# Three attention steps of TensorE issued as one task from the seventh chunk on, and fewer filler matmuls

## The chip, the core and the metric

The kernel runs on one core of a Trainium2 chip. The metric is device microseconds of one execution. The kernel before takes 482.16 us, the median of 3 runs (481.86 to 482.75). Everything is in one program on the core's engines: TensorE (PE, with its weight loads shown apart as PEld), VectorE (DVE), ScalarE (ACT), GpSimd (POOL), and the DMA queue that SyncE (SP) issues to.

## What is computed

Three layers, on 4 batches of 768 tokens with 384 channels (8 heads of 48). Cut to what matters:

```python
# 1. linear attention with decay, per batch and head
for t in range(768):
    cur = einsum('d,e->de', u * k[t], v[t])
    y[t] = r[t] @ (state + cur)
    state = w[:, None] * state + einsum('d,e->de', k[t], v[t])
# 2. gated MLP with a product over tokens
h = gelu(x @ w_in);  u, v = halves of h (512 each)
v_n = (v - mean) / sqrt(var + 1e-6) * g_ln
x = x + (u * (w_sg @ v_n + b_sg)) @ w_out
# 3. gated convolution
gate = sigmoid(causal conv of x, 5 taps per channel)
out = (gate * (x @ w_val)) @ w_out2
```

## The kernel before

The attention runs in 24 chunks of 128 tokens (chunk i is chunk i % 6 of batch i // 6). For each chunk TensorE does these steps, with the names that the rows use:

- T (`att_T`, L536): eight transposes, r and k of the chunk, each into its own PSUM bank; DVE and ACT scale and copy them out as `rT` and `kT`.
- S (`att_S`, L557): the scores, 8 products `kT` by `rT` with 48 rows contracted, into two PSUM banks. DVE masks them into two tiles `sc` (L565).
- KV (`att_KV`, L579): the chunk's state product, 8 products of k and v, 48 x 48 each. DVE adds the old state (L588), ACT decays it (L594).
- Y (`att_Y`), three parts into one bank: four transposes of the diagonal term `dv` (L612), the old state times `rT` (L619), and scores times v (L624), 8 products with 48 output rows. ACT copies the bank out (L637), and a DMA writes and re-reads it in the layout of the next layer.

L557 uses 48 rows of the array (its operands are 48 partitions high), L624 and L579 fill 48 of its columns; every other matmul of the kernel uses 112 or 128 rows and columns. A float32 matmul appears in the trace as two records, so that the 8 products of L624 are "x16" there.

The two other layers are matmuls in three passes (`three`, L778 to L780), since each float32 operand is split into a high and a low part: V and U (x by w_in, tile names `win`), SG (the product over tokens, `wsg` and `vh`, in f16), O1 (`wout`), VAL (`w_val`) and O2 (`w_out`). They are called the MLP below.

All instructions of a program are laid down in advance by a planner (`go`, L146), which keeps a clock of its own with an assumed duration for every step. There are two streams of PE tasks, attention and MLP, each a list of generators; a `yield` says how long the next piece of a task is taken to last, which results it waits for, and which PSUM banks or buffers it takes. Up to WA = 3 attention tasks and WM = 4 MLP tasks are open at once, the first ready one of each stream is a candidate, and `choose` takes the attention's as long as its share of PE time is under a goal. When neither is ready, the planner moves its clock on, and before FILL_END it lays filler matmuls into the hole (L167 to L170: `onesb` by `onesb` into columns of the bank `pw`, whose other columns hold scratch of the weight conversion, L338 to L341). The work of the other engines is kept as chains of steps, and planned with the same clock. On the chip every engine then executes its own list in order, and waits by semaphore for what it needs.

The attention's tasks stand in the list in the order S(i), KV(i), T(i+1), Y(i) (`attention`, L735; ORDER = "SKTY"). Four PSUM banks `pa` serve the attention, three banks `pm` the MLP.

Of the kernel before, what the change touches and what calls it, by code (L numbers as in the profile page):

```python
# [17 lines left out]
B, H, S, D = 4, 8, 768, 48  # L18
DM = H * D
FF = 512  # L20
NCH = S // P
# [9 lines left out]
class Kern:  # L31
# [114 lines left out]
    def go(self, streams, choose):  # L146

        live = [[] for _ in streams]
        self.done = [0.0] * len(streams)
        while True:  # L150
            for n, (gens, window) in enumerate(streams):
                while len(live[n]) < window and gens:
                    g = gens.pop(0)
                    live[n].append([g, next(g)])
            if not any(live):
                return
            times = [[self.when(t[1][2], t[1][1], self.now) for t in ts] for ts in live]
            ready = [next((i for i, t in enumerate(ts) if t is not None and t <= self.now), None) for ts in times]
            n = choose(ready)
            if n is None:  # L160
                best = self.next_step()
                soon = [t for ts in times for t in ts if t is not None]
                if best is not None:
                    soon.append(max(best[0][0], self.now))
                assert soon, ("stuck", [t[1] for ts in live for t in ts], [(c[3], c[5], c[4][0][3:]) for c in self.chains])
                t = min(soon)
                for _ in range(int((t - self.now) * (FILL0 if self.now < 14000 else FILL) / (112 if self.now < 4000 else 56)) if self.now < FILL_END and min(self.tok["pw"], default=t) <= self.now else 0):  # L167

                    nc = self.nc
                    nc.tensor.matmul(self.pw[:, TH:], self.onesb, self.onesb, start=True, stop=True)  # L170
                self.now = self.pe_end = t
                self.advance(self.now)
                continue
            i = ready[n]
            g, (ns, after, taken) = live[n][i]
            self.take(taken)
            self.pe_end = self.now + ns
            req = next(g, None)
            if req is None:
                live[n].pop(i)  # L180
            else:
                live[n][i][1] = req
            self.done[n] += ns
            self.now = self.pe_end
            self.advance(self.now)
# [338 lines left out]
    def att_T(self, i):  # L524

        nc = self.nc
        res = self.kr[i] = [None, None]
        for n, (src, tab, tag) in enumerate(((self.rp, self.tabR, "rT"), (self.ks, self.tabK, "kT"))):
            old = [("S", i - 1)] if i and n else [("Y", i - 2)] if i > 1 else []

            done = n and i
            yield 430, [("ld", i) if not n else ("kS", i) if i else "k0"] + ([("dT", i - 2)] if i > 1 else []), ["pa"]
            pt = self.ps_a()
            sv = (src[(i + (not i)) % 2] if n else src[i % NL]).rearrange("t h d -> t (h d)")
            for p in range(NP):
                nc.tensor.transpose(pt[:HR, p * P:(p + 1) * P], sv[:, p * P:p * P + HR], self.ident)  # L536
            pv = pt[:HR, :].rearrange("d (p t) -> d p t", t=P)

            def evac(e, pv=pv, tab=tab, tag=tag, n=n, done=done):
                dst = self.wp.tile([HR, NP, P], F32, tag=tag, name=self.nm(tag), bufs=1 if n else 2)  # L540
                if done:
                    e.copy(dst, pv)
                else:
                    e.tensor_mul(dst, pv, tab)  # L544
                res[n] = dst

            self.chain((tag, i), ("A", 620.0, evac, [], ["pa"]) if done else ("V", 660.0, evac, [], ["pa"]), after=old + [("tabR", "tabK")[n]], prio=pr(i))
        self.mark(("T", i))

    def att_S(self, i):  # L550
        nc = self.nc
        yield 1100, [("rT", i), ("kT", i)], ["pa", "pa"]
        rT, kT = self.kr[i]
        pA, pB = self.ps_a(), self.ps_a()
        for p in range(NP):
            for ps, r0 in ((pA, 0), (pB, 64)):
                nc.tensor.matmul(ps[:, p * P:(p + 1) * P], kT[r0:r0 + D, p, :], rT[r0:r0 + D, p, :], start=True, stop=True)  # L557
        self.mark(("S", i))
        mb = self.mask.unsqueeze(1).to_broadcast([P, NP, P])
        parts = self.scores[i] = []  # L560
        for n, ps in enumerate((pA, pB)):

            def masked(e, ps=ps):
                t = self.wp.tile([P, NP, P], F32, tag="sc", name=self.nm("sc"), bufs=2)
                e.tensor_mul(t, ps.rearrange("s (p t) -> s p t", t=P), mb)  # L565
                parts.append(t)

            self.chain(("sc", i, n), ("V", 602.0, masked, ["sc"], ["pa"]), after=[("Y", i - 1)] if i else [], prio=pr(i))

    def att_KV(self, i):  # L570

        nc = self.nc
        c = i % NCH
        yield 520, [("kS", i), ("lv", i)], ["pa"]
        kS, vt = self.kS.get(i), self.vt[i]
        pk = self.ps_a()
        for p in range(NP):
# [26 lines left out]
    def att_Y(self, i):  # L604

        nc = self.nc
        b, c = divmod(i, NCH)
        yield 430, [("D", i)], ["pa"]
        py = self.ps_a()
        dv = self.dvp[i % 2].rearrange("t h d -> t (h d)")  # L610
        for p in range(NP):
# [2 lines left out]
        rT = self.kr[i][0]  # L614
        if c:
            yield 880, [("kv", i - 1)], []
            T = self.T[i % 2]
            for p in range(NP):
                nc.tensor.matmul(py[:HR, p * P:(p + 1) * P], T[:, p, :], rT[:, p, :], start=False, stop=False)  # L619
        yield 1000, [("sc", i, 0), ("sc", i, 1)], []  # L620
        sc = self.scores.pop(i)
        for p in range(NP):
            for j, r0 in ((0, 0), (1, 64)):
# [2 lines left out]
        self.mark(("Y", i))  # L626
        self.give("sc", 2)
        self.x_rows(b, c, py[:HR], self.xd[i])

    def x_rows(self, b, c, py, scr):  # L630

# [103 lines left out]
    def attention(self):  # L735

        out = [self.att_T(0)]
        n = B * NCH
        for i in range(n):
            step = {  # L740
                "S": [self.att_S(i)] + ([] if i else [self.tables_state()]),
                "K": [self.att_KV(i)] if i % NCH != NCH - 1 else [],
                "T": [self.att_T(i + 1)] if i + 1 < n else [],
                "Y": [self.att_Y(i)],
            }
            for k in ORDER:
                out += step[k]
        return out + [self.count()]
# [385 lines left out]
def pr(i):  # L1134

    return 0 if i < NCH else PR_A
# [1 line left out]

PR_A, PR_V, PR_V0, PR_U, PR_SG, PR_REST = 1, 0.05, -1, 0.2, 0.8, 2
PR_PS = 1  # L1140
ORDER = "SKTY"
AFTER_SG, AFTER_SM, AFTER_CW = 6, 6, 9
WA, WM = 3, 4
NW = 3
# [9 lines left out]
HOLD_G, HOLD_S, TURN = 200.0, 0.0, 1280.0  # L1154
HOLD = {"gelu": HOLD_G, "sigmoid": HOLD_S}
FILL, FILL0 = 0.4, 0.8
FILL_END = 130000.0
TAIL = [(1, 0, 0), (1, 0, 1), (1, 0, 2), (0, 1, 0), (0, 1, 1), (0, 1, 2), (2, 0, 0), (2, 0, 1), (1, 1, 0), (1, 1, 1), (1, 1, 2), (2, 0, 2), (2, 1, 0), (2, 1, 1), (2, 1, 2)]
W_LEAST, W_MOST = 0.75, 1.0
N_OK = HR * NP  # L1160
# [42 lines left out]
```

## Time and profile before

| | |
|---|---|
| median of 3 runs | 482.16 us |
| the profiled execution | 481.0 us, of it 479.3 us span |
| PE busy | 453.2 us (95%) |
| DVE busy | 344.0 us (72%) |
| ACT, POOL busy | 208.1 us (43%), 175.1 us (37%) |
| chain that ended last | PE 77%, DVE 11%, issue 2%, ACT 2%, POOL 2% |

All parts that follow speak of the profiled execution, whose span is the time between its first and its last instruction. Matmuls are pipelined: a row's duration reaches beyond the start of the next row, so what a matmul costs on PE is the distance from its start to the next start. A row of the timeline merges instructions of one kind that follow each other; its count is at the end. Behind some rows stands the idle time before it and which instruction ended that idle time, inferred from semaphores.

### The profile page before, as it was taken

How to read it: one execution, taken by the hardware profiler on the slowest of the kernel's cores; microseconds unless marked ns; L12 is line 12 of the kernel's file. 1: busy time of each engine (PE TensorE's matmuls, PEld its weight loads, DVE VectorE, ACT ScalarE, POOL GpSimd, SP SyncE). 2: the span in 40 equal slices, each digit the busy share in tenths (PEclk: the TensorE clock that was granted, in tenths of full speed). 3: DMA queues.
4: the chain of work that ended last, by engine and by line, in shares of the span. 5: the costliest groups of instructions: out<-in, count | busy, mean ns of one | idle time of the engine just before them, and what ended most of it. 6: DMA issues, size and time to landing. Idle time of an engine off the chain costs nothing.

```text
span 479.3 us, 8929 instructions
## 1 busy us (share of the span) xinstructions
PE 453.2 (95%) x3423; PEld 380.2 (79%) x3423; DVE 344.0 (72%) x693; ACT 208.1 (43%) x446; POOL 175.1 (37%) x212
## 2 busy tenths in 40 slices
PE   6874989899999999999999999999999989999996
PEld 5763877868777988877887898887777978868796
DVE  5697789898998794536787585577368682658982
ACT  3437658643443475443351554453022354413142
POOL 5755466543465234353343353452023013200000
PEclk9799899999999999999999999999999999999999
DMA  7999775886343323313133433011001201000002
GB/s 148 226 207 314 214 163 110 148 173 199 83 83 74 109 48 93 76 36 83 34 63 80 106 86 112 21 31 34 2 1 41 92 0 51 0 2 0 1 35 72
DMA packets 116274, 41.37 MB, mean 86 GB/s; under 512 B 89345, under 2 KB 114049, under 8 KB 116225
## 3 DMA queue, kind: packets, MB, share of 16 engines
q1 hardware_dynamic: 116224, 40.73, 35.4%
q8 instruction: 29, 0.48, 0.4%
q14 instruction: 21, 0.16, 0.1%
HBM read 28.92 MB, written 9.44 MB: 80 GB/s over the span
## 4 chain that ended last, share of the span: by engine, by line
PE 77%; DVE 11%; issue 2%; ACT 2%; POOL 2%; DVEq 0%; ACTq 0%; POOLq 0%
PE pm L778 22%; PE pm L780 20%; PE pm L779 20%; PE pa L624 4%; PE pa L557 3%; PE pa L536 3%; PE pa L619 3%; PE pa L612 2%; DVE R L679 1%; PE pa L579 1%; DVE sc L565 1%; DVE S L341 1%; DVE bst L817 1%; DVE S L339 1%; DVE S L340 1%
## 5 line engine op out<-in xcount | busy, mean ns | idle before, releaser
L778 PE MATMUL pm<-wsg,vh 128*128 128x384 f16 x192 | 62.9, 328 | 0.0
L780 PE MATMUL pm<-wsg,vh 128*128 128x384 f16 x192 | 62.6, 326 | 0.0
L779 PE MATMUL pm<-wsg,vh 128*128 128x384 f16 x192 | 62.6, 326 | 0.0
L899 DVE SCALAR_TENSOR_TENSOR warm<-xf,cw,warm 128x384 f32<-128x384 f32 x72 | 44.5, 618 | 9.6 <-ACT warm L897 8.4
L565 DVE TENSOR_TENSOR sc<-pa,mask 128x512 f32<-128x512 f32 x48 | 31.5, 683 | 14.8 <-PE pa L557 13.2
L865 DVE SCALAR_TENSOR_TENSOR S<-pm,gs,b_bc 128x384 f32<-128x384 f32 x32 | 19.7, 615 | 28.1 <-PE pm L780 28.0
L520 POOL TENSOR_TENSOR dv<-v,dd 128x384 f32<-128x384 f32 x24 | 20.9, 872 | 49.6 <-DVE dd L513 47.2
L496 POOL TENSOR_TENSOR ks<-kp,tabS 128x384 f32<-128x384 f32 x24 | 25.5, 1064 | 27.6 <-PE pa L579 21.5
L778 PE MATMUL pm<-R,win 128*128 128x384 f32 x96 | 35.2, 366 | 0.0
L778 PE MATMUL pm<-R,wout 128*128 128x384 f32 x96 | 34.2, 356 | 0.0
L835 ACT ACTIVATE S<-pm 128x384 f32<-128x384 f32 x32 | 15.6, 488 | 39.7 <-PE pm L780 39.6
L843 POOL TENSOR_TENSOR R<-xf,R 128x384 fp32r<-128x384 f32 x11 | 11.1, 1010 | 59.2 <-ACT R L1131 37.7
L594 ACT ACTIVATE T<-T,W 112x112 f32<-112x112 f32 x80 | 26.6, 380 | 13.6 <-DVE T L588 13.5
L515 POOL TENSOR_TENSOR dv<-rp,kp 128x384 f32<-128x384 f32 x24 | 25.9, 1078 | 17.9 <-PE pa L612 15.9
L779 PE MATMUL pm<-R,wout 128*128 128x384 f32 x96 | 32.4, 337 | 0.0
L780 PE MATMUL pm<-R,win 128*128 128x384 f32 x96 | 32.4, 337 | 0.0
L779 PE MATMUL pm<-R,win 128*128 128x384 f32 x96 | 32.3, 336 | 0.0
L780 PE MATMUL pm<-R,wout 128*128 128x384 f32 x96 | 32.3, 336 | 0.0
L557 PE MATMUL pa<-rT,kT 48*128 48x128 f32 x384 | 28.8, 291 | 3.6 <-DVE kT L544 2.1
L557 PEld LDWEIGHTS pa<-rT,kT 48*128 48x128 f32 x384 | 24.1, 193 | 9.7 <-issue 4.0
L817 DVE BATCH_NORM_STATS2 bst<-A 128x6 f32<-128x512 f32 x24 | 16.6, 690 | 19.8 <-ACT A L816 19.7
L778 PE MATMUL pm<-win,R 128*128 128x512 f32 x72 | 30.0, 417 | 0.1
(170 smaller groups left out, 1225.4 us busy)
## 6 DMA issues: line engine op xcount, KB each, us to landing
rp<-in_r_dram SPq DMA_DIRECT2D x24, 192.0 KB, 3.5
kp<-in_k_dram SPq DMA_DIRECT2D x24, 192.0 KB, 3.8
v<-in_v_dram SPq DMA_DIRECT2D x24, 192.0 KB, 2.7
xd<-yT SPq DMA_DIRECT2D x48, 96.0 KB, 2.4
xf<-xd SPq DMA_DIRECT2D x24, 192.0 KB, 2.7
out_dram<-S SPq DMA_DIRECT2D x24, 192.0 KB, 2.0
Rst<-in_moe_w_in_dram SPq DMA_DIRECT2D x8, 384.0 KB, 6.0
Rst<-in_moe_w_out_dram SPq DMA_DIRECT2D x7, 384.0 KB, 5.3
```

The lines of the kernel that those rows point to most:

```text
L496: e.tensor_mul(t[:, :, 0:D], kp, self.tabS)
L515: self.chain(("dv", i), ("P", 956.0, lambda e: e.tensor_mul(dv, rp, kp)), after=[("ld", i)] + ([("dT", i - 2)] if i > 1 else []), prio=pr(i))
L520: ("P", 788.0, lambda e: e.tensor_mul(dv, self.vt[i], x["dd"].unsqueeze(2).to_broadcast([P, H, D]))),
L557: nc.tensor.matmul(ps[:, p * P:(p + 1) * P], kT[r0:r0 + D, p, :], rT[r0:r0 + D, p, :], start=True, stop=True)
L565: e.tensor_mul(t, ps.rearrange("s (p t) -> s p t", t=P), mb)
L594: return lambda e: e.activation(tnew[:, p, :], tnew[:, p, :], AF.Copy, scale=self.W[:, p:p + 1])
L778: nc.tensor.matmul(ps, lh, rh, start=m == 0, stop=False)
L779: nc.tensor.matmul(ps, lh, rl, start=False, stop=False)
L780: nc.tensor.matmul(ps, ll, rh, start=False, stop=m == total - 1)
L817: ("V", 602.0, lambda e: e.bn_stats(st, ge)),
L865: ("V", 529.0, lambda e: e.scalar_tensor_tensor(t, pg[:, :TH], self.gs[:, d:d + 1], self.b_bc[:, ts], ALU.mult, ALU.add), [], ["pm"]),
L899: eng.scalar_tensor_tensor(t, row[:, j:j + TH], self.cw[:, e, j:j + 1], t, ALU.mult, ALU.add)
```

## The change

From chunk JOIN = 6 on, Y(i)'s last part (scores times v), KV(i) and S(i+1) are one piece of one task: it waits for everything that the three need, and issues the 8 + 8 + 8 products without anything between. `att_S` is a task of its own up to chunk 6, and `att_KV` up to chunk 5. The last chunk of a batch has no KV, and the last chunk of all has no S behind it. For later chunks T(i) waits for Y(i-2) where it waited for the transposes of `dv` of chunk i-2, and the transposes of `dv` of chunk i wait for Y(i-1). Fillers are laid only while the planner's clock is under 9 us (it was 130 us), and no longer ask whether `pw` is free.

```diff
--- before.py
+++ after.py
@@ -164,7 +164,7 @@
                     soon.append(max(best[0][0], self.now))
                 assert soon, ("stuck", [t[1] for ts in live for t in ts], [(c[3], c[5], c[4][0][3:]) for c in self.chains])
                 t = min(soon)
-                for _ in range(int((t - self.now) * (FILL0 if self.now < 14000 else FILL) / (112 if self.now < 4000 else 56)) if self.now < FILL_END and min(self.tok["pw"], default=t) <= self.now else 0):
+                for _ in range(int((t - self.now) * (FILL0 if self.now < 14000 else FILL) / (112 if self.now < 4000 else 56)) if self.now < FILL_END else 0):
 
                     nc = self.nc
                     nc.tensor.matmul(self.pw[:, TH:], self.onesb, self.onesb, start=True, stop=True)
@@ -529,7 +529,7 @@
             old = [("S", i - 1)] if i and n else [("Y", i - 2)] if i > 1 else []
 
             done = n and i
-            yield 430, [("ld", i) if not n else ("kS", i) if i else "k0"] + ([("dT", i - 2)] if i > 1 else []), ["pa"]
+            yield 430, [("ld", i) if not n else ("kS", i) if i else "k0"] + ([("Y" if i > JOIN + 1 else "dT", i - 2)] if i > 1 else []), ["pa"]
             pt = self.ps_a()
             sv = (src[(i + (not i)) % 2] if n else src[i % NL]).rearrange("t h d -> t (h d)")
             for p in range(NP):
@@ -548,8 +548,11 @@
         self.mark(("T", i))
 
     def att_S(self, i):
-        nc = self.nc
         yield 1100, [("rT", i), ("kT", i)], ["pa", "pa"]
+        self.S_products(i)
+
+    def S_products(self, i):
+        nc = self.nc
         rT, kT = self.kr[i]
         pA, pB = self.ps_a(), self.ps_a()
         for p in range(NP):
@@ -568,10 +571,13 @@
             self.chain(("sc", i, n), ("V", 602.0, masked, ["sc"], ["pa"]), after=[("Y", i - 1)] if i else [], prio=pr(i))
 
     def att_KV(self, i):
+        yield 520, [("kS", i), ("lv", i)], ["pa"]
+        self.KV_products(i)
+
+    def KV_products(self, i):
 
         nc = self.nc
         c = i % NCH
-        yield 520, [("kS", i), ("lv", i)], ["pa"]
         kS, vt = self.kS.get(i), self.vt[i]
         pk = self.ps_a()
         for p in range(NP):
@@ -605,7 +611,7 @@
 
         nc = self.nc
         b, c = divmod(i, NCH)
-        yield 430, [("D", i)], ["pa"]
+        yield 430, [("D", i)] + ([("Y", i - 1)] if i > JOIN else []), ["pa"]
         py = self.ps_a()
         dv = self.dvp[i % 2].rearrange("t h d -> t (h d)")
         for p in range(NP):
@@ -617,7 +623,14 @@
             T = self.T[i % 2]
             for p in range(NP):
                 nc.tensor.matmul(py[:HR, p * P:(p + 1) * P], T[:, p, :], rT[:, p, :], start=False, stop=False)
-        yield 1000, [("sc", i, 0), ("sc", i, 1)], []
+
+        kv = i >= JOIN and c != NCH - 1
+        s = i >= JOIN and i + 1 < B * NCH
+        yield (
+            1000 + 390 * kv + 980 * s,
+            [("sc", i, 0), ("sc", i, 1)] + ([("kS", i), ("lv", i)] if kv else []) + ([("rT", i + 1), ("kT", i + 1)] if s else []),
+            ["pa"] * (kv + 2 * s),
+        )
         sc = self.scores.pop(i)
         for p in range(NP):
             for j, r0 in ((0, 0), (1, 64)):
@@ -626,6 +639,10 @@
         self.mark(("Y", i))
         self.give("sc", 2)
         self.x_rows(b, c, py[:HR], self.xd[i])
+        if kv:
+            self.KV_products(i)
+        if s:
+            self.S_products(i + 1)
 
     def x_rows(self, b, c, py, scr):
 
@@ -738,8 +755,8 @@
         n = B * NCH
         for i in range(n):
             step = {
-                "S": [self.att_S(i)] + ([] if i else [self.tables_state()]),
-                "K": [self.att_KV(i)] if i % NCH != NCH - 1 else [],
+                "S": ([self.att_S(i)] if i <= JOIN else []) + ([] if i else [self.tables_state()]),
+                "K": [self.att_KV(i)] if i < JOIN and i % NCH != NCH - 1 else [],
                 "T": [self.att_T(i + 1)] if i + 1 < n else [],
                 "Y": [self.att_Y(i)],
             }
@@ -1138,7 +1155,7 @@
 
 PR_A, PR_V, PR_V0, PR_U, PR_SG, PR_REST = 1, 0.05, -1, 0.2, 0.8, 2
 PR_PS = 1
-ORDER = "SKTY"
+ORDER, JOIN = "SKTY", 6
 AFTER_SG, AFTER_SM, AFTER_CW = 6, 6, 9
 WA, WM = 3, 4
 NW = 3
@@ -1154,7 +1171,7 @@
 HOLD_G, HOLD_S, TURN = 200.0, 0.0, 1280.0
 HOLD = {"gelu": HOLD_G, "sigmoid": HOLD_S}
 FILL, FILL0 = 0.4, 0.8
-FILL_END = 130000.0
+FILL_END = 9000.0
 TAIL = [(1, 0, 0), (1, 0, 1), (1, 0, 2), (0, 1, 0), (0, 1, 1), (0, 1, 2), (2, 0, 0), (2, 0, 1), (1, 1, 0), (1, 1, 1), (1, 1, 2), (2, 0, 2), (2, 1, 0), (2, 1, 1), (2, 1, 2)]
 W_LEAST, W_MOST = 0.75, 1.0
 N_OK = HR * NP
```

Two places in PE's list and one in DVE's show what this moves. First PE in the middle of the program, about chunk 15 (in the trace of before at 213 to 221 us). Of before, `sc`/`v` is Y (L624), `rT`/`kT` is S (L557), `v`/`ks` is KV (L579); the left-out rows are their other products and MLP matmuls:

```order
L780 MATMUL pm_2671<-wsg_182,vh_2186 128x384
L624 MATMUL pa_2659<-sc_2574,v_2309 48x128
...
L778 MATMUL pm_2671<-wsg_182,vh_2185 128x384
...
L557 MATMUL pa_2732<-rT_2631,kT_2651 128x128
...
L778 MATMUL pm_2726<-wsg_182,vh_2185 128x384
...
L579 MATMUL pa_2770<-v_2530,ks_124 48x48 x8
L778 MATMUL pm_2783<-R_2191,win_96 128x384
```

The same place in the changed kernel, whose lines have other numbers (L637 is Y, L585 KV, L560 S, L795 to L797 the MLP):

```order
L797 MATMUL pm_2764<-wsg_182,vh_2183 128x384
L637 MATMUL pa_2755<-sc_2659,v_2479 48x128
...
L585 MATMUL pa_2800<-v_2479,ks_124 48x48 x8
L560 MATMUL pa_2809<-rT_2760,kT_2746 128x128
...
L795 MATMUL pm_2823<-R_2189,win_96 128x384
```

Where Y, S and KV stood between MLP matmuls one by one, they now follow each other. The second place is PE's list at the first chunk, with the fillers (`onesb`), of before:

```order
L579 MATMUL pa_315<-v_143,ks_123 48x48 x8
L612 MATMUL pa_327<-ident,dv_131 112x128 x4
L170 LDWEIGHTS onesb
L170 MATMUL warm<-onesb 128x128
L536 MATMUL pa_337<-ident,rp_118 112x128 x4
...
L624 MATMUL pa_327<-sc_334,v_143 48x128
L170 LDWEIGHTS onesb
...
L536 MATMUL pa_373<-ident,ks_124 112x128 x4
```

and of the changed kernel:

```order
L585 MATMUL pa_315<-v_143,ks_123 48x48 x8
L618 MATMUL pa_327<-ident,dv_131 112x128 x4
L536 MATMUL pa_336<-ident,rp_118 112x128 x4
L637 MATMUL pa_327<-sc_324,v_143 48x128
...
L536 MATMUL pa_365<-ident,ks_124 112x128 x4
```

All eight fillers of this place are gone. Three more go later (two ahead of chunk 3's `dv`, one in the T of chunk 8); the 69 ahead of this place stay. The third place is DVE's list at the turn from the third to the last batch (in the trace of before at 390 to 396 us), where the last gate of the convolution is finished: `warm` are its taps (L899), `bst`, `mv`, `rs`, `A` and `vh` normalise the next batch's v, and the `S` by `pm` (L929) applies the gate. Before:

```order
L899 SCALAR_TENSOR_TENSOR warm<-xf_3100,cw,warm 128x384 x2
L817 BN_STATS bst_4566<-A_4565 128x6
L899 SCALAR_TENSOR_TENSOR warm<-xf_3100,cw,warm 128x384
L800 BN_AGGR mv_4567<-bst_4566 128x2
L801 TENSOR_SCALAR rs_4568<-mv_4567 128x1
L811 TENSOR_SCALAR A_4565<-A_4565,mv_4567,rs_4568 128x512
L821 CAST vh_4544<-A_4565 128x512
L929 TENSOR_TENSOR S_4603<-pm_4518,S_4603 128x384
```

and in the changed kernel:

```order
L916 SCALAR_TENSOR_TENSOR warm<-xf_3119,cw,warm 128x384 x2
L834 BN_STATS bst_4562<-A_4561 128x6
L817 BN_AGGR mv_4563<-bst_4562 128x2
L818 TENSOR_SCALAR rs_4564<-mv_4563 128x1
L946 TENSOR_TENSOR S_4573<-pm_4507,S_4573 128x384
```

Two instructions of the normalisation no longer stand ahead of the gate.

## Rows read from the trace of the kernel before

**Rows 1.** Stretches: us, each engine's busy time, granted clock, DMA share, GB/s.

```profile
75.00:143.00 68.00, 65.45 (x568) 52.67 (x566) 61.68 (x125) 36.67 (x82) 34.08 (x36) 1.00 0.64 139
143.00:387.00 244.00, 243.92 (x1818) 204.79 (x1819) 165.51 (x315) 98.99 (x203) 87.27 (x99) 1.00 0.25 60
387.00:396.00 9.00, 6.82 (x35) 5.80 (x34) 7.80 (x19) 5.89 (x9) 1.89 (x3) 1.00 0.00 0
```

**Rows 2.** PE's timeline at Y: start us, us, line, tiles, partitions, type, count.

```profile
213.33 1.08 PE L624 MATMUL pa<-sc,v 128*48 128x128 f32 x16
214.35 0.34 PE L778 MATMUL pm<-wsg,vh 128*128 128x384 f16 x1
```

**Rows 3.** PE's timeline at S.

```profile
216.60 0.33 PE L779 MATMUL pm<-wsg,vh 128*128 128x384 f16 x1
216.76 0.33 PE L780 MATMUL pm<-wsg,vh 128*128 128x384 f16 x1
217.01 1.16 PE L557 MATMUL pa<-rT,kT 48*128 48x128 f32 x16
218.11 0.34 PE L778 MATMUL pm<-wsg,vh 128*128 128x384 f16 x1
218.28 0.33 PE L779 MATMUL pm<-wsg,vh 128*128 128x384 f16 x1
```

**Rows 4.** PE's timeline at KV, and behind it the MLP in f32.

```profile
220.65 0.56 PE L579 MATMUL pa<-v,ks 128*48 128x48 f32 x16
221.15 0.44 PE L778 MATMUL pm<-R,win 128*128 128x384 f32 x1
221.42 0.34 PE L779 MATMUL pm<-R,win 128*128 128x384 f32 x1
221.60 0.34 PE L780 MATMUL pm<-R,win 128*128 128x384 f32 x1
```

**Rows 5.** PE's timeline where KV follows Y at once.

```profile
176.70 1.08 PE L624 MATMUL pa<-sc,v 128*48 128x128 f32 x16
177.61 0.53 PE L579 MATMUL pa<-v,ks 128*48 128x48 f32 x16
178.07 0.44 PE L778 MATMUL pm<-w_out,R 128*128 128x384 f32 x1
```

**Rows 6.** PE's timeline where KV follows S at once.

```profile
99.66 1.16 PE L557 MATMUL pa<-rT,kT 48*128 48x128 f32 x16
100.75 0.56 PE L579 MATMUL pa<-v,ks 128*48 128x48 f32 x16
```

**Rows 7.** PE's timeline at the six fillers of the first chunk.

```profile
19.06 0.51 PE L170 MATMUL warm<-onesb 128*128 128x128 bf16 x6
19.41 0.60 PE L536 MATMUL pa<-ident,ks 128*112 128x128 f32 x4
```

**Rows 8.** PE's timeline at the two later fillers.

```profile
45.97 0.37 PE L170 MATMUL warm<-onesb 128*128 128x128 bf16 x2 [4.40 <-DVE S L341]
```

**Rows 9.** Waits of PE: us in total, times, longest us.

```profile
PE pm L778 <- DVE S L929: 2.1, 1, 2.1
PE pa L557 <- ACT kT L542: 1.5, 2, 0.7
PE pa L612 <- ACT yT L637: 1.2, 1, 1.2
```

**Rows 10.** Stretches in the first chunks, columns as in Rows 1.

```profile
14.00:16.00 2.00, 2.00 (x26) 1.69 (x25) 1.35 (x3) 0.83 (x3) 1.78 (x3) 0.50 1.00 310
18.00:20.00 2.00, 2.00 (x28) 1.64 (x26) 0.35 (x1) 0.82 (x3) 1.72 (x2) 0.88 0.62 173
```

**Rows 11.** PE's timeline at the wait of the T of chunk 8.

```profile
85.21 0.62 PE L536 MATMUL pa<-ident,ks 128*112 128x128 f32 x4 [2.00 <-DVE mv L800]
```

**Rows 12.** DVE's timeline ahead of the last gate of the third batch.

```profile
394.10 0.55 DVE L811 TENSOR_SCALAR A<-A,mv,rs 128x512 f32<-128x512 f32 x1 [0.66 <-POOL rs L804]
394.68 0.43 DVE L821 CAST vh<-A 128x512 f16<-128x512 f32 x1
395.02 0.55 DVE L929 TENSOR_TENSOR S<-pm,S 128x384 f32<-128x384 f32 x1
```

More of the change, by code (lines that the diff above doesn't have):

```diff
@@ L550, in att_S @@
     def att_S(self, i):
+        yield 1100, [("rT", i), ("kT", i)], ["pa", "pa"]
+        self.S_products(i)
+    def S_products(self, i):
         nc = self.nc
-        yield 1100, [("rT", i), ("kT", i)], ["pa", "pa"]
         rT, kT = self.kr[i]
```

## The prediction

> **What bounds the kernel now.** I read the page's shares first, then the stretches, then PE's waits, then PE's timeline at the steps that move. The stretches [rows 1] show two regimes. From 143 to 387 us PE has 243.92 us of work in 244.00: whatever PE no longer has to do there comes off the end, and DVE, at 165.51 of 244, is not near. From 75 to 143 us PE is idle for 2.55 us of 68, but DVE is busy for 61.68 (91%): there PE and DVE run neck and neck. From 387 to 396 us there is a hole of 2.18 us. So the main question is what PE's own time becomes, and the second is what the front, up to 143 us, does with it.
>
> PE's timeline shows a price that no duration column tells. Two f16 matmuls of the MLP start 0.16 us apart (216.60, 216.76), but S starts 0.25 us behind the last of them [rows 3]: entering a step that uses 48 rows costs 0.09 us. S then holds PE for 1.10 us, and the f16 matmuls behind it are 0.17 apart, 0.01 more than usual. KV takes 0.50 us to the next matmul [rows 4], and the first f32 matmul behind it takes 0.27 us (221.15 to 221.42) where the next takes 0.18: leaving into f32 costs a further 0.09 to 0.10. Y between f16 matmuls takes 1.02 us [rows 2]. Where KV follows Y at once, Y takes only 0.91 us and KV only 0.46 [rows 5]: both fill 48 columns, and nothing is paid between them. Where KV follows S at once, S takes 1.09 us [rows 6], as much as ahead of an MLP matmul: between the two small shapes the price is paid as between small and full.
>
> **The change part by part.** The instructions of Y, KV and S stay the same in number; what goes are entrances and exits. I counted in both lists of PE what stands ahead of each of the 24 Y, 20 KV and 24 S, and behind.
>
> - Entrances from a full-size matmul: 56 before, 30 now. 26 x 0.09 [rows 3] = 2.3 us.
> - Y with KV right behind it: 2 before, 16 now. 14 x (1.02 - 0.91) [rows 2, 5] = 1.5 us.
> - KV with Y right ahead: also 2 and 16. 14 x (0.50 - 0.46) [rows 4, 5] = 0.6 us.
> - Exits into f32 matmuls of the MLP: 28 before, 15 now. 13 x 0.10 [rows 4] = 1.3 us. Exits into f16: 14 and 5, 9 x 0.01 [rows 3] = 0.1 us. Exits into transposes, 13 and 10, I count at nothing.
> - S right behind KV, 15 times, stands nowhere in the trace of before. From below, it is entered without a price, as KV behind Y: 15 x 0.10 = 1.5 us more gain. From above, it costs two prices: 1.5 us less. I take the one price that KV pays into an MLP matmul and that S pays into KV [rows 4, 6], so the term is zero.
>
> PE has 5.8 us less to do (4.3 to 7.3). The Trainium skill, in "TensorEngine Tiling (Array Packing)", section Tiling Modes, says that a change of tiling mode drains the engine while a change of tile within one mode does not. By that rule KV to S, 64 columns to 64 rows, would pay one drain, which leaves the sum at 5.8; entered free it would be 7.3. The trace agrees as far as it goes: nothing between Y and KV, 0.09 to 0.10 us wherever the shape changes.
>
> The fillers: 11 go. Six take 0.35 us (19.06 to 19.41) [rows 7], 0.06 each, so the eight of the first chunk take 0.5 us. What follows there soon waits for the copy of kT by ACT [rows 9], itself behind PE's transposes, and for others; I take half, 0.25 us, with 0 and 0.5 as ends. The two at 45.97 us waited 4.40 us for DVE's use of the bank [rows 8], which looks like a large gain and is none: the transposes behind them went on waiting 1.2 us for ACT's copy of yT [rows 9], which ACT reaches in its own order whatever PE does. Zero. The last one stands ahead of a 2.00 us wait [rows 11]: zero.
>
> That wait itself, for a bank that the mask of S(7) frees (the row names the instruction that ended nearest), is in the part that is ordered anew. S(7) now comes ahead of the nine MLP matmuls that it followed, and its masks stand ahead of the weight split of DVE; on the other hand the copy of Y(6) by ACT now stands behind two weight steps. It may go wholly (-2.0) or grow by a mask's time (+0.7); I take it as unchanged.
>
> The hole at 393 us: PE waits 2.1 us for the last gate [rows 9]. On DVE the gate's product at 395.02 stood behind two steps of the next batch, one of which waited 0.66 us for POOL [rows 12]. Both are now behind it, from 394.10 to 395.02 about 0.9 us. Against that, the 9 matmuls of U that covered part of the chain (9 x 0.18 = 1.6 us [rows 4]) are now behind the wait. Ends -2.1 and +0.7; I take -0.5.
>
> New waits: the joined piece needs rT and kT of the next chunk within 2.4 us of the chunk's Y (0.09 + 0.91 + 0.46 to S). In the long middle there are T, MLP, dv, MLP, the state product and MLP between kT's transposes and S, several us, so nothing is late. In the front some of chunks 6 to 10 come with no MLP in between, and DVE is at 91%. Waits of this kind took 0.7 us each before [rows 9]. I charge 5 joins x 0.2 = 1.0 us (0 to 3.5). The changed waits of T(i) for Y(i-2) and of dv(i) for Y(i-1) only write down what PE's order holds already: zero. SP's queue issues the same DMAs; the write of yT(6) moves back with ACT's copy, and with it the transposes of w_sg behind it; if they come late for the products that use them, that is part of the 1.0.
>
> Sum: -5.8 - 0.25 - 0.5 + 1.0 = -5.55 us. The profiled execution took 481.0 us, so it would take 475.4; against the median of 482.16, 1.2 us higher, 476.6. I forecast 476.6.
>
> **Rivals.** *The front keeps its share.* DVE at 91% up to 143 us [rows 1] sets the pace, and PE's shorter steps become waits. 5 of the 17 joins lie there, 5.8 x 5 / 17 = 1.7 us of the gain; with the charge of new waits at 1.7 rather than 1.0 the time is 479.0. For it: DVE's share. Against it: PE idled only 2.55 us in 68.
>
> *Every join waits for kT: slower.* Y, KV and S are one block, and PE executes in order: if ACT's copy of kT or DVE's rT is late, all MLP matmuls behind S wait too, which they could pass before. It decides from 5.8 / 17 = 0.34 us per join; at the 0.7 us that the two waits for kT took [rows 9], 17 x 0.7 - 5.8 = +6.1 us, 488. Against it: in the middle several us lie between the transposes of kT and S.
>
> *The clock stays low at the start.* At 14 to 16 us the granted clock is 0.50 (1.2 GHz), at 18 to 20 us 0.88, with PE busy throughout [rows 10]; the clock rises to 2.4 GHz while the eight fillers run. Without them the rise may come later: if PE does 4 us of work at half rate, it loses up to 4 us, less what later waits absorb: 476.6 + 2.4 = 479. The rule that speaks for it is in "TensorE: Matmul & The Clock Gate" of the Trainium skill, Part 1: throttled is the default, and activity lifts it. Against it: without the fillers PE is no less busy there, since its own work moves up into their place.
>
> *It does not do what it says.* The price at the borders is a matter of weight loads that appear elsewhere, so that the time stays at 482. Against it: the f16 start distances behind Y and S are back at 0.16 to 0.17 at once.
>
> **How the numbers follow.** Forecast 0.58, with 474.3 to 478.3 as its own range (the price of KV to S and half of the idle terms). Front 0.22, at 479.0, to 480.8. Clock 0.07, at 479. No effect, or gain and new waits about equal, 0.06. Slower 0.07. The range 474.0 to 480.4 leaves out both last cases, the lower end where KV to S is free, and the tip of the front case. About 0.2% (1 us) is what a measurement of this kernel tells from no change, so faster is under 481.2: 0.58 + 0.22 + 0.07, less a little of the front case, 0.86. Same 0.07, slower 0.07.
>
> **What would show it.** Right: in the profile after, Y, KV and S in one row of 2.46 us or so (0.91 + 0.46 + 1.09), 15 times; PE's busy time 5 to 6 us lower; PE full from 143 us on. The hole near the last batch at 1.5 us or less. Wrong: S starting more than 0.5 us behind the start of KV, which prices the unseen border; waits of S for kT, rT or of Y for masks of more than 0.3 us each over most joins; a granted clock under 1 beyond 20 us where it was 1; or more than 3 us of new idle time ahead of 143 us.

## The result, and the profile after

The changed kernel takes 476.13 us in the median of 6 runs (475.7 to 480.19), the kernel before 482.01 us on the same chip: a ratio of 0.9889, with a 95% interval of 0.9861 to 0.9916. The forecast was 476.6, its range 474.0 to 480.4. The profiled execution took 476.46 us with a span of 474.5 (before: 481.0 and 479.3). Run twice more, the same kernel gave 0.9934 (0.9909 to 0.9959) and 0.9842 (0.9802 to 0.9882). The experiments show that most of this spread goes with PE's clock.

First the joined task, in PE's timeline of the kernel after (start us, us, engine, line, operation, tiles, partitions, shape, type, count). Lines have moved: Y is L637, KV L585, S L560, the MLP L795 to L797.

```profile
206.90 0.33 PE L797 MATMUL pm<-wsg,vh 128*128 128x384 f16 x1
207.16 1.08 PE L637 MATMUL pa<-sc,v 128*48 128x128 f32 x16
208.07 0.53 PE L585 MATMUL pa<-v,ks 128*48 128x48 f32 x16
208.53 1.16 PE L560 MATMUL pa<-rT,kT 48*128 48x128 f32 x16
209.62 0.34 PE L795 MATMUL pm<-wsg,vh 128*128 128x384 f16 x1
209.80 0.33 PE L796 MATMUL pm<-wsg,vh 128*128 128x384 f16 x1
```

Read starts, not durations. Y's start lies 0.26 behind the last f16 matmul where those lie 0.16 apart: one entrance of 0.10, where before each of the three paid one (S in [rows 3]; in the trace of before the Y at 119.16 us and the KV at 126.35 us also start 0.25 behind an f16 matmul). Y then takes 0.91, KV 0.46 and S 1.09, 2.46 us together, and S behind KV costs what S cost ahead of an MLP matmul.

Then the stretches (us, busy time of PE, PE's weight loads, DVE, ACT and POOL, granted clock, DMA share, GB/s), against [rows 1]; the last one is new.

```profile
75.00:143.00 68.00, 64.39 (x556) 53.89 (x556) 61.71 (x122) 35.82 (x78) 32.97 (x36) 0.97 0.65 137
143.00:387.00 244.00, 243.97 (x1847) 209.65 (x1845) 167.48 (x327) 104.38 (x212) 85.98 (x99) 1.00 0.26 61
387.00:396.00 9.00, 7.92 (x41) 7.21 (x42) 3.71 (x8) 6.30 (x10) 1.01 (x2) 1.00 0.20 68
138.00:141.00 3.00, 3.00 (x17) 2.84 (x17) 2.50 (x5) 2.97 (x7) 1.57 (x2) 0.54 0.56 108
```

The long middle is full, as before. The hole near the last batch shrinks from 2.18 us idle to 1.08. From 75 to 143 us PE idles 3.61 us in place of 2.55. From 138 to 141 us its clock is 0.54, nearly all of it at 1.2 GHz, where before it was 1.00. By the page PE's busy time falls from 453.2 to 448.0 us, although half of some 3.3 us is new in it by the lower clock, and the span falls by 4.8: the gain is work that PE no longer has; its idle time grows by some 0.4 in all.

PE's waits, in its timeline (in brackets the idle time and what ended it):

```profile
47.14 0.65 PE L618 MATMUL pa<-ident,dv 128*112 128x128 f32 x2 [6.02 <-ACT yT L654]
83.93 0.50 PE L797 MATMUL pm<-win,R 128*128 128x512 f32 x1 [0.84 <-DVE R L696]
96.90 0.29 PE L618 MATMUL pa<-ident,dv 128*112 128x128 f32 x1 [0.88 <-DVE sc L568]
135.43 0.65 PE L536 MATMUL pa<-ident,rp 128*112 128x128 f32 x4 [0.55 <-ACT yT L654]
137.42 1.07 PE L536 MATMUL pa<-ident,ks 128*112 128x128 f32 x4 [1.34 <-DVE sc L568]
389.33 0.44 PE L795 MATMUL pm<-w_out,R 128*128 128x384 f32 x1 [1.08 <-DVE S L946]
```

The two fillers are gone from 46 us [rows 8], and the transposes there wait 6.02 us for ACT in one piece where it was 4.40 for the fillers, 0.37 of fillers and 1.24 behind them. The 2.00 us at 83 us, for a bank [rows 11], are gone: the T of chunk 8 starts at 81.15 us without a wait. What stands at 83.93 is another wait of 0.84 us, of an MLP matmul for DVE's split of x (`R`), which comes behind the masks of S(7) now. At 134.88 to 137.42 us stands a new wait of 1.89 us with 0.65 us of work in the middle, in the T of the twelfth chunk. It wants two banks; ACT's copy of yT ends the first wait, DVE's mask of S(10) the longer one. DVE's own timeline says why the mask is late:

```profile
135.15 1.27 DVE L916 SCALAR_TENSOR_TENSOR warm<-xf,cw,warm 128x384 f32<-128x384 f32 x2
136.33 0.34 DVE L594 TENSOR_TENSOR T<-pa,T 48x192 f32<-48x192 f32 x1
136.60 0.67 DVE L568 TENSOR_TENSOR sc<-pa,mask 128x512 f32<-128x512 f32 x1
```

S(10) was done by 132.6 us. DVE came to its first mask 4 us later, having been busy since 127.5 us, but for a wait of 0.3 us, with words of the weights, splits of MLP operands, the convolution and a step of the state.

### The profile page after: what moved, and what is told of

It reads as the page before. It is cut to its first block, busy times and chain, and to the rows that moved or that the text cites. A ratio compares the mean times of both kernels' runs of the same rounds, so it can differ in the third digit from the quotient of the medians.

```text
span 474.5 us, 8899 instructions
## 1 busy us (share of the span) xinstructions
PE 448.0 (94%) x3412; PEld 383.0 (81%) x3412; DVE 343.8 (72%) x697; ACT 208.5 (44%) x443; POOL 172.0 (36%) x211
## 4 chain that ended last, share of the span: by engine, by line
PE 74%; DVE 10%; ACT 3%; DMA 2%; SPq 2%; POOL 2%; issue 1%; DVEq 0%; POOLq 0%; ACTq 0%
PE pm L795 20%; PE pm L797 19%; PE pm L796 19%; PE pa L637 4%; PE pa L560 3%; PE pa L625 3%; PE pa L536 3%; PE pa L618 2%; DVE sc L568 1%; DMA st<-in_moe_w_sg_dram 1%; PE pa L585 1%; DVE R L696 1%; DMA xf<-xd 1%; SPq L392 1%; DVE S L341 1%
## 5 line engine op out<-in xcount | busy, mean ns | idle before, releaser
L795 PE MATMUL pm<-wsg,vh 128*128 128x384 f16 x192 | 62.8, 327 | 0.0
L797 PE MATMUL pm<-wsg,vh 128*128 128x384 f16 x192 | 62.6, 326 | 0.0
L795 PE MATMUL pm<-R,win 128*128 128x384 f32 x96 | 34.6, 360 | 0.0
L795 PE MATMUL pm<-R,wout 128*128 128x384 f32 x96 | 33.7, 351 | 0.0
L560 PE MATMUL pa<-rT,kT 48*128 48x128 f32 x384 | 28.9, 291 | 3.9 <-DVE kT L544 2.1
L797 PE MATMUL pm<-R,wout 128*128 128x384 f32 x96 | 32.4, 337 | 0.0
L797 PE MATMUL pm<-R,win 128*128 128x384 f32 x96 | 32.3, 337 | 0.0
L1148 ACT CAST R<-S 128x384 fp32r<-128x384 f32 x32 | 16.3, 513 | 32.2 <-DVE S L884 17.9
L560 PEld LDWEIGHTS pa<-rT,kT 48*128 48x128 f32 x384 | 24.2, 193 | 6.6 <-ACT kT L542 2.4
L795 PE MATMUL pm<-win,R 128*128 128x512 f32 x72 | 29.4, 408 | 0.0
```

What stands on the lines that cost most here:

```text
L795: nc.tensor.matmul(ps, lh, rh, start=m == 0, stop=False)
L797: nc.tensor.matmul(ps, ll, rh, start=False, stop=m == total - 1)
```

## A measure for differences under 1%

Executions of one kernel differ by 1%, and so does the mean granted clock that each run lists with its span. The mean of their product is steadier. On one chip the kernel before had, in its 17 runs, spans whose product with the clock has a mean of 472.7 us with a standard error of 0.2, though its times run from 480.54 (clock 0.986) to 485.52 (0.977). On two other chips it was 472.4 and 472.5. It is the span that the work would take if all of it had run at 2.4 GHz, roughly, since idle time counts too. Single products still scatter: over the runs of before on one chip their standard deviation is 0.65 to 0.8 us where that of the times is 1.1 to 1.5, but over the 7 runs of the changed kernel's second set both are 1.2. And the product takes off too much: in the runs of before the span is 3.4 us longer where the mean clock is 0.01 lower, and a constant product would ask for 4.9. Taken off at 3.4, the differences from the changed kernel in all its runs move by at most 0.6 us. The table has it beside the medians (mean over the runs, standard errors 0.1 to 0.5).

```
                    median   before, same chip   ratio (95%)               span x clock   runs
changed kernel      476.13   482.01              0.9889 (0.9861..0.9916)   466.9           6
  again             478.67   481.46              0.9934 (0.9909..0.9959)   467.1           7
  third time        474.45   481.92              0.9842 (0.9802..0.9882)   466.0           4
join alone          475.96   482.59              0.9863 (0.9836..0.9890)   466.0           6
fillers alone       482.60   482.59              1.0005 (0.9989..1.0022)   472.2          13
S ahead of KV       478.20   482.59              0.9896 (0.9868..0.9923)   469.6           6
Y and KV joined     478.44   482.59              0.9911 (0.9885..0.9937)   469.1           6
halves              478.76   481.46              0.9956 (0.9934..0.9979)   469.9          12
joins from 13th     475.37   481.46              0.9869 (0.9843..0.9896)   466.5           6
T(11) filled        475.83   481.46              0.9889 (0.9861..0.9918)   467.0           6
one join less       479.39   481.92              0.9931 (0.9903..0.9958)   467.3          12
13th, old fillers   476.15   481.92              0.9867 (0.9827..0.9906)   466.7           4
join, filled        474.99   481.92              0.9844 (0.9805..0.9883)   466.1           4
```

Before against the changed kernel this is 472.5 against 466.8 (mean over its 17 runs): 5.7 us of gain, where the sum of the prediction had 5.55.

## The experiments

**The two parts apart.** The changed kernel with the fillers of before, and the kernel before with the new rule for fillers alone.

```
-FILL_END = 9000.0
+FILL_END = 130000.0      (and the condition on the bank's token is back)
```

> The joined task alone; the fillers follow the rule of before. My theory: the join makes all of the gain but the 0.25 us of the fillers, so 5.6 us below before, 0.2 to 0.3 us above the changed kernel: 476.4 us where before is 482.0. Rival: the fillers matter (the 4.40 us wait of two of them for DVE, or the clock), then the join alone leaves 478 us or more.

> The kernel before with the new rule for the fillers alone. My theory: 0 to 0.5 us below before, 481.75 where before is 482.0; PE's wait at 41 to 47 us stays about 6 us long, since the transposes there wait for ACT's copy of yT. Rival 1: the fillers' wait for DVE was real and 2 us or more go. Rival 2: without the fillers the clock stays low for longer in the first 20 us, and it is 1 us or more slower than before.

The join alone gives all of it: 475.96, and 466.0 by the product, which is 0.8 below the changed kernel and not 0.2 to 0.3 above as expected; the two were not measured side by side, and this is left open. In its profile, as in that of before, the clock does not fall between 75 and 470 us; with the same fillers PE's busy time is 447.4 us on its page where before's is 453.2: 5.8 less. The fillers alone give nothing that these runs can tell (1.0005). The 0.25 us that I had put down for them is too small to be seen, and neither rival shows. In the profile with the fillers alone, PE's timeline at 46 us is that of the changed kernel, one wait of 6 us for ACT:

```profile
46.40 0.86 PE L612 MATMUL pa<-ident,dv 128*112 128x128 f32 x3 [6.01 <-ACT yT L637]
```

So the 4.40 us that the fillers waited for DVE was worth nothing.

**The price at the borders, by order.** Within the joined task S stands ahead of KV.

```
-        if kv:
-            self.KV_products(i)
         if s:
             self.S_products(i + 1)
+        if kv:
+            self.KV_products(i)
```

> The changed kernel with one edit: within the joined task the next chunk's scores stand ahead of the state product, so that Y to S and S to KV are two changes of shape where Y to KV to S was one. Same tasks, same instructions. Theory of the price at the borders: 15 joined tasks x (0.10 + 0.04) = 2.1 us more of PE's time than the changed kernel: 478.2 where that is 476.1, and Y takes 1.01 us in place of 0.91 in the joined tasks. Rival (the gain comes from fewer tasks and waits, not from shapes): the same as the changed kernel within 0.5 us.

It took 478.2, as forecast; by the product 2.8 us more than the changed kernel (2.4 at 3.4 us per 0.01 of clock). The timeline shows one border more:

```profile
208.91 0.33 PE L797 MATMUL pm<-wsg,vh 128*128 128x384 f16 x1
209.17 1.08 PE L637 MATMUL pa<-sc,v 128*48 128x128 f32 x16
210.18 1.16 PE L560 MATMUL pa<-rT,kT 48*128 48x128 f32 x16
211.27 0.56 PE L585 MATMUL pa<-v,ks 128*48 128x48 f32 x16
211.77 0.34 PE L795 MATMUL pm<-wsg,vh 128*128 128x384 f16 x1
```

Y takes 1.01 (0.91 in the changed kernel), S 1.09, KV 0.50 (0.46): 2.60 us in place of 2.46, and 15 x 0.14 = 2.1 us. The rest fits idle time: PE idles 4.65 us from 75 to 143 us in this profile, 1.0 more. The price can also be read where no clock and no wait blurs it. Between the Y of chunk 11 and that of chunk 22 PE has 1372 matmul records in both kernels, with nine joined tasks that hold all three parts (PE's timeline, the changed kernel, then this one):

```profile
154.14 1.08 PE L637 MATMUL pa<-sc,v 128*48 128x128 f32 x16
326.80 1.08 PE L637 MATMUL pa<-sc,v 128*48 128x128 f32 x16
```

```profile
155.90 1.08 PE L637 MATMUL pa<-sc,v 128*48 128x128 f32 x16
329.70 1.08 PE L637 MATMUL pa<-sc,v 128*48 128x128 f32 x16
```

That is 172.66 against 173.80 us: 1.14 more for nine tasks, 0.13 each. The two other profiles of the changed kernel have 172.65 and 172.63. The rival, that the tasks and not the shapes count, falls.

**The price at the borders, doubled.** Half of KV, half of S, the other half of KV, the other half of S.

```
-        if kv:
-            self.KV_products(i)
-        if s:
-            self.S_products(i + 1)
+        if kv and s:
+            k, n = self.KV_halves(i), self.S_halves(i + 1)
+            next(k), next(n)
+            next(k, None), next(n, None)
...
```

> The changed kernel with one edit: in each of the 15 joined tasks that hold all three parts, half of KV, half of S, the other half of KV, the other half of S. Same instructions and tasks, two more changes of shape in each. Theory of the price at the borders: KV to S and S to KV at 0.11 and 0.10 us, 15 x 0.21 = 3.1 us slower than the changed kernel, 479.2. Rival (the price stands once at the entry of a task and not at each change): within 0.5 us of the changed kernel.

Its median is 478.76, and that of the changed kernel on the same chip 478.67: by the medians alone the rival's "within 0.5 us" came true. But the changed kernel's clocks were lower there (0.977 to 0.986 against 0.982 to 0.987), and by the product the kernel of halves is 3.1 us above the changed kernel in all its runs, 2.8 above it on this chip. The timeline decides: the rival falls, and the price of a change was set too low:

```profile
207.45 0.35 PE L596 MATMUL pa<-v,ks 128*48 128x48 f32 x8
207.73 0.71 PE L566 MATMUL pa<-rT,kT 48*128 48x128 f32 x8
208.37 0.38 PE L596 MATMUL pa<-v,ks 128*48 128x48 f32 x8
208.69 0.71 PE L566 MATMUL pa<-rT,kT 48*128 48x128 f32 x8
209.34 0.34 PE L810 MATMUL pm<-wsg,vh 128*128 128x384 f16 x1
```

KV and S take 0.28 + 0.64 + 0.32 + 0.65 = 1.89 us where they took 1.55: 0.34 per task, 0.17 for each of the two added changes and not 0.10. All 15 tasks show these distances. From the Y of chunk 11 to that of chunk 22 it is 175.62 us where the changed kernel takes 172.66:

```profile
152.87 1.08 PE L648 MATMUL pa<-sc,v 128*48 128x128 f32 x16
328.49 1.08 PE L648 MATMUL pa<-sc,v 128*48 128x128 f32 x16
```

So the middle pays in full, 2.96 us for nine tasks. 15 x 0.34 would be 5.1 us; that the product shows 3.1 leaves next to nothing for the five tasks in the front. Waits took up part of their 1.7 us, for PE idles 3.06 us from 75 to 143 us in this profile where it was 3.61; the rest was not tried apart. The Trainium skill, "TensorEngine Tiling (Array Packing)", section Tiling Modes, has a change of mode drain the engine; both kernels agree as far as a price shows it: each change of the small shape costs 0.13 to 0.17 us, and Y to KV, of one shape, nothing.

**Y and KV joined, S apart.**

```
-        s = i >= JOIN and i + 1 < B * NCH
+        s = False
-"S": ([self.att_S(i)] if i <= JOIN else [])
+"S": [self.att_S(i)]
```

> Y and KV joined from the seventh chunk on, S a task of its own. Theory of the price at the borders: 46 entrances in place of 56 before and 30 in the changed kernel; by the counts of its order PE has 3.3 us less than before to do and 2.7 us more than the changed kernel. S can move again, so the new idle time at 134 to 137 us (1.9 us) and the clock of 0.50 behind it (3.4 us at half rate, 1.7 us of work) may go: 475.5 to 478.8 us, PE's busy time at 449 to 450. Rival (S in the join is what helps, since it keeps S from waiting): 481 or more.

478.44, within the range and under the rival's 481. PE's busy time is 451.4, over the 449 to 450 expected; some 1.7 us of it comes from a fall of the clock late in the program, shown below. By the product it is 2.3 us above the changed kernel, close to the 2.7 that its borders say. From 75 to 143 us PE idles 1.37 us: the wait at 134 to 137 us is gone. The hole near the last batch is back, though, at its old size, with a stretch at 1.2 GHz behind it (PE's timeline, then DVE's, then the stretches of this kernel):

```profile
392.06 0.44 PE L795 MATMUL pm<-w_out,R 128*128 128x384 f32 x1 [2.04 <-DVE S L946]
```

```profile
390.53 0.55 DVE L828 TENSOR_SCALAR A<-A,mv,rs 128x512 f32<-128x512 f32 x1 [0.66 <-POOL rs L821]
391.11 0.43 DVE L838 CAST vh<-A 128x512 f16<-128x512 f32 x1
391.45 0.55 DVE L946 TENSOR_TENSOR S<-pm,S 128x384 f32<-128x384 f32 x1
```

```profile
390.00:393.00 3.00, 0.96 (x6) 0.94 (x6) 1.86 (x4) 0.78 (x2) 2.19 (x3) 1.00 0.00 0
393.00:397.00 4.00, 4.00 (x15) 3.79 (x14) 0.20 (x1) 1.91 (x4) 0.00 (x0) 0.57 0.27 98
```

The two steps of the next batch stand ahead of the gate's product on DVE again, with the 0.66 us for POOL, as before [rows 12].

**Is the clock of 137 us the order's or the execution's?** The changed kernel again; and with the rT transposes of T(11) issued four times, which fills the wait.

> The changed kernel once more, as the measure for the three beside it. Its time again 476 us (ratio 0.986 to 0.992). If the clock of 0.50 at 137 to 141 us belongs to its order of work, it is there again; if it is an accident of one execution, PE's wait of 1.9 us at 134 to 137 us is there and the clock is 1.00.

```
-            for p in range(NP):
+            for p in [*range(NP)] * (4 if i == 11 and not n else 1):
                 nc.tensor.transpose(pt[:HR, ...
```

> The changed kernel with 12 matmuls more: the four transposes of rT of the twelfth chunk (135.43 us) are issued four times, with the same result, so that 1.3 us of PE's wait for the mask (136.09 to 137.42) is filled with work. PE's idle time falls by 1.3 us and the end is the same. Theory: the clock falls behind such waits in some executions (137 to 141 us in the profile of the changed kernel, 1.6 us of work); with PE kept busy it never does here, and the median is 0 to 0.8 us below the changed kernel. Rival: the clock falls there all the same, or the copies delay rT and the time is 0.5 us or more above.

In the profile of the second set the waits are there (0.43 and 1.34 us, 1.77 in place of 1.89) and the clock is not lower:

```profile
138.00:141.00 3.00, 2.51 (x26) 2.40 (x28) 2.94 (x6) 2.21 (x6) 1.37 (x2) 1.00 0.82 156
```

So one order of work meets both clocks. Its 7 runs had mean clocks of 0.977 to 0.986 and times of 476.29 to 479.38; the median of 478.67 and the ratio of 0.9934 lie outside what was expected. Filled, the six runs were at 0.983 to 0.988 and the median 2.8 us lower on the same chip, more than the 0.8 expected, at the same product (467.0): the difference goes with the clock. That the filling did it isn't settled, for in its third set the changed kernel, unfilled, ran at 0.985 to 0.987.

**Where the joins pay.** Joins from the 13th chunk on (`JOIN = 12`).

> The changed kernel with the joins from the 13th chunk on in place of the 7th. By the counts of its order PE has 1.15 us more at its borders than the changed kernel. Ahead of 143 us the waits should be those of before (2.55 us from 75 to 143 us in place of 3.61). Theory: 476.0 to 476.5, the same as the changed kernel, since what the five joins in the front save comes back there as waits for DVE. Rival (the front keeps its gain): 477.3 or more.

475.37, a little under the range. That is 3.3 us below the changed kernel's median on this chip (478.67), but with higher clocks; by the product it is 466.5, 0.3 below the changed kernel, which has 1.15 us less at its borders. Its stretch ahead of the middle has the idle time of before:

```profile
75.00:143.00 68.00, 65.46 (x568) 52.99 (x566) 61.36 (x123) 36.90 (x83) 33.02 (x35) 1.00 0.61 137
37.00:40.00 3.00, 3.00 (x31) 2.50 (x29) 1.32 (x3) 2.65 (x6) 3.00 (x4) 0.50 0.92 225
```

2.54 us idle against 3.61: what the joins of the front save at the borders (1.15) comes back as waits for DVE (1.07). The second row is a fall of the clock at another place, behind waits of 1.19 and 0.73 us that every one of these kernels has.

**One join less.** S(10) is a task of its own again.

```
-        s = i >= JOIN and i + 1 < B * NCH
+        s = i >= JOIN and i + 1 < B * NCH and i != 9
```

> The changed kernel with one join less: the scores of the 11th chunk (131 us) are a task of their own again. One border more, 0.15 us by the counts. Theory: PE's wait of 1.9 us at 134 to 137 us comes from that join (its two banks are masked late by a busy DVE), so it falls to 0.7 us or less, the clock does not fall behind it, and the median is 1 to 3 us below the changed kernel. Rival: DVE sets the pace there and the wait comes back at the next chunk; the same within 0.5 us.

This failed. 479.39 is not below the changed kernel on that chip (474.45, the third run in the table) but 4.9 us above, the two intervals clear of each other. PE's timeline and the stretches:

```profile
136.61 0.62 PE L536 MATMUL pa<-ident,ks 128*112 128x128 f32 x4 [0.69 <-DVE T L594]
139.21 0.67 PE L618 MATMUL pa<-ident,dv 128*112 128x128 f32 x2 [1.98 <-DVE sc L568]
```

```profile
138.00:141.00 3.00, 1.79 (x9) 1.79 (x10) 2.97 (x6) 2.48 (x4) 0.97 (x2) 0.53 0.37 72
141.00:145.00 4.00, 4.00 (x41) 3.63 (x42) 3.11 (x6) 0.77 (x2) 1.57 (x3) 0.50 0.02 4
```

The wait went from T to the transposes of dv and, with the 0.69 us ahead of it, grew to 2.67 us; DVE sets the pace there, as the rival had it. And the clock fell in it: 0.50 from a little behind 138 us to 145 us, and ten of the twelve runs have mean clocks of 0.974 to 0.981. By the product it is 467.3, 0.5 above the changed kernel in all its runs and 1.3 above it on this chip (466.0, standard error 0.45); 2 to 3 of the 4.9 us go with the clock, at 3.4 us per 0.01 or by the product.

**The best of both, and the measure.**

> The changed kernel a third time, as the measure on this chip. Theory: its span times its mean granted clock is 466.5 to 467.5 us again, whatever its median; the spread of single executions is a matter of where the clock fell.

> Joins from the 13th chunk on and the fillers of before: the version that the runs so far point to. Fillers change nothing within 0.5 us, so 475 to 476 us where before is 481.5, 0 to 3 us below the changed kernel.

> The join alone with the fillers of before, and the transposes of rT of the twelfth chunk four times over, which keep PE busy in the wait at 136 us. Theory: the clock does not fall at 137 us, and the fillers cost nothing: 475.0 to 476.0 us where before is 481.5. Rival (the fall comes at another wait instead): no lower than the changed kernel.

474.45, 476.15 and 474.99, with products of 466.0, 466.7 and 466.1. The product of the first is 0.5 below the 466.5 to 467.5 expected, about its standard error of 0.45. Neither of the two versions beats the changed kernel here: the second is 1.7 us above it where 0 to 3 below was expected. The third has the outcome of its rival, no lower than the changed kernel, though in its profile the clock is 1.00 from 75 us to the end of the middle. The stretch of the changed kernel's profile, with a wait of 1.43 us ahead of it (where it was 1.89), is at full clock once more:

```profile
138.00:141.00 3.00, 3.00 (x53) 2.63 (x53) 2.21 (x5) 2.93 (x5) 2.96 (x4) 1.00 0.08 17
```

## Why the prediction was right

The forecast of 476.6 lies 0.5 us from the first median, and that closeness is luck: the medians of the three sets lie 4.2 us apart. The range holds all three, and the gain by the product, 5.7, is what the prediction's mechanism has to answer for.

**The borders, -5.8: right.** Every price stands in the timeline after to 0.01 us: 0.10 for the entrance, 0.91 for Y, 0.46 for KV, 1.09 for S, 2.46 for the task. S right behind KV, the shape change that the trace of before did not have, costs one price, as taken. Two kernels that put changes of shape back at the same number of tasks lost time, 2.8 and 3.1 us by the product, 1.14 and 2.96 us in the nine tasks between the Y of chunks 11 and 22.

**The fillers, -0.25: nothing measurable.** The two at 46 us were rightly priced at zero. Of the eight of the first chunk half came back as taken: S waits 0.24 us for ACT's copy of kT at 20.59 us, where it didn't wait before.

**The hole, -0.5: twice that.** It shrank from 2.07 to 1.08 us. The step's two ends were -2.1 and +0.7, and I took a value near the middle. That DVE's two steps of the next batch no longer stand ahead of the gate's product is what shrank it, but they are not behind it on DVE, as the prediction had it: ACT does them.

```profile
388.46 0.15 DVE L818 TENSOR_SCALAR rs<-mv 128x1 f32<-128x1 f32 x1
388.72 0.56 DVE L946 TENSOR_TENSOR S<-pm,S 128x384 f32<-128x384 f32 x1
389.84 0.82 ACT L826 ACTIVATE A<-A,nm,rs 128x512 f32<-128x512 f32 x1 [1.15 <-POOL nm L822]
390.69 0.62 ACT L838 CAST vh<-A 128x512 f16<-128x512 f32 x1
```

With Y and KV joined alone they stand ahead of the gate on DVE again, and it stays 2.04; in the two profiles with joins from the 13th chunk it is 1.08. So it hangs on S being in the join, in the middle.

**The bank's wait at 83 us, 0: it went wholly,** the end of -2.0 that the prediction had named and priced at nothing. The masks of S(7) come early enough now. But PE reaches the MLP matmuls behind it earlier too, and one of them waits 0.84 us for DVE's split of x, which stands behind those masks: 1.2 us net. With joins from the 13th chunk on, the bank's wait is there again (2.03 us).

**New waits, +1.0: the place was wrong and the size too small.** They were expected as S waiting for kT or rT. No such wait is new in a join: those of S all stand ahead of 40 us. The joined task takes three banks in one piece, DVE frees those of S late, and the tasks behind it wait for a bank: 0.88 us at 96 us and 1.89 us at 134 to 137. Together 2.8 us; less the 1.2 at 83 us and the 0.6 of small waits at 137 to 143 us that went, 1.0 net. So the idle terms came out by errors that cancel, which is luck.

**The front keeps its share: its mechanism is what happens,** at a smaller price than the rival had. Joins from the 13th chunk on do as well as joins from the 7th.

**The clock at the start: did not happen.** It rises between 17 and 18 us in the changed kernel (0.57 there, then 1.00), between 18 and 19 before (0.50, then 0.75), there while Y runs from 17.66 us and ahead of the six fillers at 19.06. But the clock fell at 137 us in the profiled execution, which no step had: some 3.3 us of PE's work at 1.2 GHz, which costs half of that, 1.6 us. A clock under 1 behind 20 us where it was 1 was one of the signs of being wrong that the prediction named; it came, and the gain in work was there all the same. The Trainium skill says in "TensorE: Matmul & The Clock Gate", Part 1, that the throttled clock is the default and that activity lifts it; the trace agrees at the start (0.50 at 14 to 16 us, 1.00 at 18 to 20). Why one order of work keeps its clock in one execution and loses it in the next, no run here shows.

**Joins that wait for kT, slower: no.** Nothing in the middle waits: 243.97 us of work in 244.00.

## What to carry to other kernels

Where an engine is full, count what its tasks pay when they change shape, in start-to-start distances: matmuls of small shapes put side by side made up the gain of 5.7 us of 482 here, and gave all of it without an instruction less. Expect little of it where another engine sets the pace: in the front, under DVE, the saving came back as waits, and behind some of the longer waits the clock fell besides. And before two versions are compared at 0.5%, multiply span by granted clock: the medians of one kernel lay between 474.45 and 478.67 us, the products between 466.0 and 467.1. Below 1 us the product doesn't decide either; start distances over a stretch in which the engine never waits do (172.63 to 172.66 us in three profiles).

## What was not expected of the hardware

- TensorE's clock falls behind waits of PE of some 2 us in the midst of a busy stretch, in some executions and not in others of the same kernel with nearly the same waits. Seen: 0.54 at 138 to 141 us behind 1.89 us of waits (changed kernel, one profile of three; with 1.77 and 1.43 us the others stay at 1.00), 0.50 at 138 to 145 us in and behind 2.67 us, 0.57 at 393 to 397 us behind 2.04 us, and 0.50 at 37 to 40 us behind 1.19 and 0.73 us, which the other profiles have at 1.00 there. Before's wait of 2.07 us at 393 us did not bring it, nor did one of 2.17 us at 138 to 140 us with S ahead of KV. What decides stays open.
- Splitting a run of 16 small matmuls costs more than the border read at its ends: 0.17 us for each change in the kernel of halves, against 0.10 to 0.14 where whole runs change places.
